# A gate of softplus and erf as two ScalarE activations instead of exp, ln and a tanh of a polynomial

## The chip, the cores and the metric

The kernel runs on one core of one Trainium2 chip. The time is the device time of one execution in microseconds (us), a median over several. The profile's span, from the first to the last instruction, is about 1.8 us shorter than the time of the same execution; against the median the difference varies, since one execution alone is profiled.

The engines in the profile's words: PE is TensorE's matmuls, PEld its weight loads, DVE is VectorE, ACT is ScalarE, POOL is GpSimd. PSUM is the memory that the kernels' matmuls write their results to. The granted clock is the share of TensorE's full clock that the profile shows as granted.

## The reference

A retention layer (a linear recurrence by head) feeds a feed-forward layer whose activation is h · erf(softplus(h)).

```python
# q, k, v: (4, 8, 768, 64)     w_in: (512, 2048)   w_out: (2048, 512), weights in float64
state = gamma * state + outer(k[t], v[t])          # for every batch and head
y[t]  = scale * q[t] @ state
x = y, as (3072, 512)
h = x @ w_in
sp = np.maximum(h, 0.0) + np.log1p(np.exp(-np.abs(h)))
g = h * erf(sp)
return (g @ w_out).astype(np.float32)
```

## The kernel before

Retention is done in 24 chunks of 128 tokens, each in four steps: transposes, scores, output, state. The feed-forward part takes 512 tokens at a time, and of them groups of FG blocks of 128 hidden features. The weights come as float64 bits and are converted on the chip. The issue order is written out by hand, so each engine works through its own instructions in program order, whatever else would be ready: in the conversion shown below VectorE idled 1.44 us for GpSimd, with the copy of a hidden block next in its queue; TensorE had ended the block at 109.26 us, and its copy began at 111.68.

```python
FG = 2  # blocks of 128 hidden features that go through the activation together
# ... [cut]
    # convert(): two shifts-and-masks, a top word, a scaled low word on VectorE, and then
    nc.scalar.activation(normal, hi.bitcast(F32), AF.Abs)
    nc.gpsimd.tensor_scalar(normal, normal, F64_LEAST, 1.0, op0=ALU.is_ge, op1=ALU.mult)
    nc.gpsimd.tensor_tensor(lowf, topf, lowf, op=ALU.add)
    nc.gpsimd.tensor_tensor(to, lowf, normal, op=ALU.mult)      # [views cut]
# ... [cut]
    # ret_out(): state and value matmuls alternate for each pair of heads
    for hp in range(HP):
        if c:
            nc.tensor.matmul(p[:, hp, :], state[:, hp, :], QD[j][:, hp, :], start=True, ...)
        for s in range(2):
            nc.tensor.matmul(p[s*D:(s+1)*D, hp, :], XT["v", j][:, 2*hp+s, :], AM[j][:, s, hp, :], ...)
    nc.scalar.copy(XC[m][:, :, i * C : (i + 1) * C], p)
# ... [cut]
def hidden(g, u):        # 4 matmuls of 512 columns into PSUM, then
    nc.scalar.copy(HS[g][:, u * TCH : (u + 1) * TCH], p)

def cap(g):              # VectorE: e = min(h, 4)
def softplus(g):         # ScalarE Exp, Ln(1 + e); GpSimd: five operations that repair the rounding
def poly(g):             # VectorE: square, first step, then
    for a in ERF_R[-2:0:-1]:
        nc.vector.scalar_tensor_tensor(z, z, a, x2, op0=ALU.add, op1=ALU.mult)
def erf_tanh(g):         # ScalarE Tanh
def gated(g):            # GpSimd: g = h * tanh
def project(g):          # 4 x FG matmuls of 512 columns into 4 PSUM banks
```

The stages of one group are spread over four rounds of the loop: cap and softplus of group g, polynomial of g−1, tanh and gating of g−2, projection of g−3.

## Time and profile before

| | before |
|---|---|
| time | 1345.3 us (1343.5 to 1346.2, four runs) |
| span of the profile | 1342.4 us |
| VectorE busy | 1204.3 us, 90% |
| GpSimd busy | 876.8 us, 65% |
| TensorE busy | 905.4 us, 67%; mean granted clock 0.819 |
| ScalarE busy | 396.7 us, 30% |

Busy time of TensorE is not its work. Overlapping records count once: the 768 of the projection last 659 ns each, 506 us in all, and count as 385.6 us. And a lower clock stretches them: at half clock (granted 0.50, from 706.2 to 709.5 us) the weight loads of the projection start 0.85 us apart, at 1.00 (from 709.6 us on) 0.43. A safer measure is the interval between starts in a stretch without gaps. The page also cuts the span into 40 slices; a digit is the busy share in tenths, and in the last line the granted TensorE clock. These are slices of the kernel before, 33.6 us each:

```profile
PE   6861537347196597939669669857966969739645
...
DVE  4668998989899899998999999999999999999995
...
PEclk9676868768597897979789779969878979859877
```

VectorE is at 8 or 9 from the fourth slice on, but for the last. TensorE swings between 1 and 9, and its clock goes largely with it: where TensorE shows 3 or less, the clock shows 5 to 7, and where it shows 9, the clock shows 8 or 9.

### The profile page before, as it was taken

What the parts mean: (1) busy time and instruction counts of PE and PEld (TensorE: products, weight loads), DVE (VectorE), ACT (ScalarE), POOL (GpSimd) and SP (SyncE); (2) the same over time, 40 slices, a digit from 0 to 9 for tenths busy, and PEclk for the clock granted to TensorE, in tenths of its full rate; (3) what the DMA queues carried; (4) which work ended last, traced back from release to release, by engine and by line L of the source; (5) the groups of instructions that cost most, each with busy time, mean ns of one, the idle gap of its engine ahead of it and who ended that gap; (6) DMA issues with size and microseconds to landing.
All of it is one profiled execution on the core that took longest, in us unless ns stands there. A gap on an engine that the chain in (4) does not pass through costs nothing.

```text
span 1342.4 us, 7959 instructions
## 1 busy us (share of the span) xinstructions
PE 905.4 (67%) x2816; PEld 449.1 (33%) x2816; DVE 1204.3 (90%) x842; ACT 396.7 (30%) x453; POOL 876.8 (65%) x410
## 2 busy tenths in 40 slices
PE   6861537347196597939669669857966969739645
PEld 4531213123043343414335334323433534314212
DVE  4668998989899899998999999999999999999995
ACT  2231122222132342423233243233323324132310
POOL 5687788887766564855756657576574666666661
PEclk9676868768597897979789779969878979859877
DMA  9531021213000210101010002000000000000000
GB/s 239 133 82 48 31 55 32 70 47 78 0 17 8 63 24 8 23 1 51 20 24 9 15 9 63 16 16 8 1 8 23 1 1 0 0 31 0 0 0 31
DMA packets 89703, 43.24 MB, mean 32 GB/s; under 512 B 76096, under 2 KB 84288, under 8 KB 89664
## 3 DMA queue, kind: packets, MB, share of 16 engines
q1 hardware_dynamic: 89664, 42.74, 12.5%
q8 instruction: 22, 0.36, 0.1%
q14 instruction: 17, 0.14, 0.0%
HBM read 36.44 MB, written 6.29 MB: 32 GB/s over the span
## 4 chain that ended last, share of the span: by engine, by line
DVE 79%; POOL 7%; PE 6%; issue 4%; ACT 2%; DMA 1%; SPq 1%; POOLq 0%; DVEq 0%
DVE xx L314 56%; DVE e L311 5%; DVE xx L312 4%; DVE e L292 4%; DVE xx L315 3%; PE r L212 3%; DVE am L220 2%; POOL low L145 2%; POOL normal L144 1%; POOL w_out_sb L147 1%; DVE qd L205 1%; ACT normal L143 1%; DMA out_dram<-osb 1%; DVE state L263 1%; PE o L331 1%
## 5 line engine op out<-in xcount | busy, mean ns | idle before, releaser
L314 DVE SCALAR_TENSOR_TENSOR xx<-xx,e 128x1024 f32<-128x1024 f32 x384 | 775.5, 2020 | 13.2
L331 PE MATMUL o<-w_out_sb,g 128*128 128x512 f32 x768 | 385.6, 659 | 75.5 <-POOL g L322 52.1
L284 PE MATMUL hp<-xT,w_in_sb 128*128 128x512 f32 x768 | 360.4, 615 | 52.1 <-ACT h L288 42.1
L322 POOL TENSOR_TENSOR g<-h,xx 128x1024 f32<-128x1024 f32 x48 | 121.2, 2525 | 295.3 <-ACT xx L318 295.3
L331 PEld LDWEIGHTS o<-w_out_sb,g 128*128 128x128 f32 x768 | 159.3, 213 | 278.8 <-issue 197.8
L212 PE MATMUL r<-qT,kT 64*128 64x128 f32 x384 | 57.3, 413 | 282.1 <-DVE qd L205 163.8
L284 PEld LDWEIGHTS hp<-xT,w_in_sb 128*128 128x128 f32 x768 | 147.6, 197 | 228.2 <-issue 172.4
L306 POOL TENSOR_TENSOR sp<-sp,xx 128x1024 f32<-128x1024 f32 x48 | 153.1, 3189 | 3.8
L305 POOL TENSOR_TENSOR xx<-xx,kept 128x1024 f32<-128x1024 f32 x48 | 152.7, 3180 | 4.0
L212 PEld LDWEIGHTS r<-qT,kT 64*128 64x128 f32 x384 | 46.7, 296 | 302.7 <-DVE qd L205 167.6
L318 ACT ACTIVATE xx<-xx 128x1024 f32<-128x1024 f32 x48 | 50.7, 1057 | 320.3 <-DVE xx L315 320.0
L302 POOL TENSOR_SCALAR xx<-e 128x1024 f32<-128x1024 f32 x48 | 78.8, 1642 | 60.2 <-ACT e L297 60.2
L288 ACT COPY h<-hp 128x512 f32<-128x512 f32 x96 | 55.6, 584 | 202.2 <-PE hp L284 191.3
L304 POOL TENSOR_SCALAR kept<-kept 128x1024 f32<-128x1024 f32 x48 | 90.0, 1876 | 4.0
L143 ACT ACTIVATE normal<-w 128x512 f32<-128x512 f32 x32 | 21.4, 667 | 237.6 <-POOL w_out_sb L147 148.6
L303 POOL TENSOR_SCALAR kept<-xx 128x1024 f32<-128x1024 f32 x48 | 86.8, 1808 | 4.0
L144 POOL TENSOR_SCALAR normal<-normal 128x512 f32<-128x512 f32 x32 | 70.2, 2194 | 23.7 <-ACT normal L143 23.7
L297 ACT ACTIVATE e<-e 128x1024 f32<-128x1024 f32 x48 | 50.5, 1053 | 100.9 <-DVE e L292 100.9
L311 DVE TENSOR_TENSOR e<-sp 128x1024 f32<-128x1024 f32 x48 | 77.8, 1621 | 0.0
L220 DVE TENSOR_TENSOR am<-r,d_in 128x512 f32<-128x512 f32 x48 | 30.9, 686 | 50.6 <-PE r L212 50.6
L145 POOL TENSOR_TENSOR low<-top,low 128x512 f32<-128x512 f32 x32 | 44.2, 1382 | 48.4 <-DVE low L142 48.4
L312 DVE TENSOR_SCALAR xx<-e 128x1024 f32<-128x1024 f32 x48 | 60.4, 1258 | 1.6
(41 smaller groups left out, 822.6 us busy)
## 6 DMA issues: line engine op xcount, KB each, us to landing
w<-in_moe_w_in_dram SPq DMA_DIRECT2D x16, 512.0 KB, 3.9
w<-in_moe_w_out_dram SPq DMA_DIRECT2D x16, 512.0 KB, 3.4
q<-in_q_dram SPq DMA_DIRECT2D x24, 256.0 KB, 3.6
k<-in_k_dram SPq DMA_DIRECT2D x24, 256.0 KB, 4.7
v<-in_v_dram SPq DMA_DIRECT2D x24, 256.0 KB, 4.3
out_dram<-osb SPq DMA_DIRECT2D x24, 256.0 KB, 2.1
d_in<-decay_in_dram SPq DMA_DIRECT2D x1, 512.0 KB, 5.0
d_q<-decay_q_dram SPq DMA_DIRECT2D x1, 256.0 KB, 5.3
```

The source lines that it names most:

```text
L144: nc.gpsimd.tensor_scalar(normal, normal, F64_LEAST, 1.0, op0=ALU.is_ge, op1=ALU.mult)
L212: nc.tensor.matmul(pp[s][:, hp, :], KT[j][s * D : (s + 1) * D, hp, :], QT[j][s * D : (s + 1) * D, hp, :], start=True, stop=True,)
L284: nc.tensor.matmul(p, w_in_sb[:, kk, ft * P : (ft + 1) * P], XC[m][:, kk, :], start=(kk == 0), stop=(kk == n_k - 1),)
L303: nc.gpsimd.tensor_scalar(kept, small, 1.0, 1.0, op0=ALU.add, op1=ALU.mult)
L304: nc.gpsimd.tensor_scalar(kept, kept, -1.0, 1.0, op0=ALU.add, op1=ALU.mult)
L305: nc.gpsimd.tensor_tensor(small, small, kept, op=ALU.subtract)
L306: nc.gpsimd.tensor_tensor(SP[g], SP[g], small, op=ALU.add)
L311: nc.vector.tensor_tensor(x2, SP[g], SP[g], op=ALU.mult)
L312: nc.vector.tensor_scalar(z, x2, ERF_R[-1], None, op0=ALU.mult)
L314: nc.vector.scalar_tensor_tensor(z, z, a, x2, op0=ALU.add, op1=ALU.mult)
L322: nc.gpsimd.tensor_tensor(G[g], HS[g], XX[g], op=ALU.mult)
L331: nc.tensor.matmul(O[m][tt], G[g][:, u * TCH + tt * P : u * TCH + (tt + 1) * P], w_out_sb[:, ft, :], start=(ft == 0), stop=(ft == n_ft - 1),)
```

## The change

The intent is to take the polynomial off VectorE and the repair off GpSimd: ScalarE has Softplus and Erf as activations, 1912 ns each for a row of 2048 elements in the profile after. Around this, six further things change: groups of four blocks instead of two, the evacuation copies from PSUM on VectorE instead of ScalarE, a shorter conversion, state matmuls before value matmuls, a pipeline one group deep, and another order of loads and conversions. With them some work changes engine: the gating product goes from GpSimd to VectorE, two small products of the retention from VectorE to GpSimd.

```diff
-FG = 2
+FG = 4
 # convert()
-        nc.scalar.activation(normal, hi.bitcast(F32), AF.Abs)
-        nc.gpsimd.tensor_scalar(normal, normal, F64_LEAST, 1.0, op0=ALU.is_ge, op1=ALU.mult)
+        nc.scalar.activation(square, hi.bitcast(F32), AF.Square)
         nc.gpsimd.tensor_tensor(lowf, topf, lowf, op=ALU.add)
-        nc.gpsimd.tensor_tensor(to, lowf, normal, op=ALU.mult)            # views cut
+        nc.vector.scalar_tensor_tensor(to, square, F64_LEAST**2, lowf,    # views cut
+                                       op0=ALU.is_ge, op1=ALU.mult)
 # retention
-            nc.scalar.copy(store[j], p)
+            nc.vector.tensor_copy(store[j], p)
-                nc.vector.tensor_tensor(QD[j], p, d_q, op=ALU.mult)
+                nc.gpsimd.tensor_tensor(QD[j], QT[j], d_q, op=ALU.mult)
-        for hp in range(HP):
-            if c: (state matmul)
-            for s in range(2): (value matmul)
-        nc.scalar.copy(XC[m][:, :, i * C : (i + 1) * C], p)
+        if c:
+            for hp in range(HP): (state matmul, start=(hp == 0))
+        for hp in range(HP):
+            for s in range(2): (value matmul, start=(not c and hp == 0))
+        nc.vector.tensor_copy(XC[m][:, :, i * C : (i + 1) * C], p)
 # feed-forward
-        nc.scalar.copy(HS[g][:, u * TCH : (u + 1) * TCH], p)
-    (cap, softplus, poly, erf_tanh)
+        nc.vector.tensor_copy(HS[g][:, u * TCH : (u + 1) * TCH], p)
+    def gate(g):
+        E[g] = act.tile([P, N], F32, name="e")
+        nc.scalar.activation(E[g], HS[g], AF.Softplus)
+        nc.scalar.activation(E[g], E[g], AF.Erf)
     def gated(g):
-        nc.gpsimd.tensor_tensor(G[g], HS[g], XX[g], op=ALU.mult)
+        for a in range(2):
+            half = slice(a * N // 2, (a + 1) * N // 2)
+            nc.vector.tensor_tensor(E[g][:, half], HS[g][:, half], E[g][:, half], op=ALU.mult)
 # loop: prologue converts 4 blocks (was 8); then, for each group
+            for u in range(FG):
+                hidden(g, u)
+                if u == 0 and g:
+                    gated(g - 1)
+                ret_step()
+                for _ in range(2):
+                    convert_piece()
+            gate(g)
+            project(g - 1)
 # [cut: order of the loads and of the pieces, w with 4 buffers, output copies all on ScalarE, the state's decay on GpSimd]
```

More of the change, by code (lines that the diff above doesn't have):

```diff
@@ L21 @@
 TCH = 512
-FG = 2
+FG = 4
 F64_LEAST = float(np.array(897 << 20, np.uint32).view(np.float32))
-H_CAP = 4.0
-ERF_R = (
-    1.128379178523394,
-    0.10277216167188301,
-    -0.00020663606065076897,
-    -0.0005953413444015755,
-    6.935073696802299e-05,
-    1.3126385158198855e-06,
-    -1.285398332234825e-06,
-    1.5565170067658438e-07,
-    -8.4325147215839e-09,
-    1.7770446978797262e-10,
-)
 @with_exitstack
@@ L88, in load @@
         b, c = divmod(j, NC)
-        for name, src in (("q", q), ("k", k), ("v", v)):
+        for name, src in (("k", k), ("q", q), ("v", v)):
             x = loads.tile([P, H, D], F32, name=name)
@@ L99 @@
     w_out_sb = const.tile([P, n_ft, d_model], F32, name="w_out_sb")
-    load(0)
-    nc.sync.dma_start(d_k, decay_k)
-    nc.sync.dma_start(d_in, decay_in)
-    nc.sync.dma_start(d_q, decay_q)
-    nc.sync.dma_start(d_s, decay_s)
     W = {}
     def load_weight(which, ft):
-        w = raw.tile([P, d_model], I64, name="w", bufs=3)
+        w = raw.tile([P, d_model], I64, name="w", bufs=4)
         if which == "in":
@@ L132, in convert @@
         low = raw.tile([P, d_model], U32, name="low")
-        normal = raw.tile([P, d_model], F32, name="normal", bufs=1)
+        square = raw.tile([P, d_model], F32, name="square")
         topf, lowf = top.bitcast(F32), low.bitcast(F32)
@@ L142, in convert @@
         nc.vector.scalar_tensor_tensor(lowf, lo, 2.0**-52, lowf, op0=ALU.mult, op1=ALU.mult)
-        nc.scalar.activation(normal, hi.bitcast(F32), AF.Abs)
-        nc.gpsimd.tensor_scalar(normal, normal, F64_LEAST, 1.0, op0=ALU.is_ge, op1=ALU.mult)
+        nc.scalar.activation(square, hi.bitcast(F32), AF.Square)
         nc.gpsimd.tensor_tensor(lowf, topf, lowf, op=ALU.add)
         g = to.shape[1]
-        nc.gpsimd.tensor_tensor(
+        nc.vector.scalar_tensor_tensor(
             to,
+            square.rearrange("p (g f) -> p g f", g=g),
+            F64_LEAST**2,
             lowf.rearrange("p (g f) -> p g f", g=g),
-            normal.rearrange("p (g f) -> p g f", g=g),
-            op=ALU.mult,
-        )
-    pieces = [("in", ft) for ft in range(n_ft // 2)]
-    for n in range(n_ft // 2):
-        pieces += [("in", n_ft // 2 + n), ("out", n)]
-    pieces += [("out", ft) for ft in range(n_ft // 2, n_ft)]
+            op0=ALU.is_ge,
+            op1=ALU.mult,
+        )
+    pieces = [("in", ft) for ft in range(FG)]
+    for n in range(n_g):
+        for u in range(FG):
+            if n + 1 < n_g:
+                pieces.append(("in", (n + 1) * FG + u))
+            pieces.append(("out", n * FG + u))
     to_load, to_convert = list(pieces), list(pieces)
@@ L167, in convert_piece @@
             load_piece()
+    load(0)
+    nc.sync.dma_start(d_k, decay_k)
+    nc.sync.dma_start(d_q, decay_q)
+    load_piece()
+    nc.sync.dma_start(d_in, decay_in)
+    nc.sync.dma_start(d_s, decay_s)
     load(1)
@@ L177 @@
     make_identity(nc, ident)
-    one = const.tile([P, 1], F32, name="one")
-    nc.vector.memset(one, 1.0)
     state = const.tile([P, HP, P], F32, name="state")
@@ L227, in ret_out @@
         p = ps_r.tile([P, HP, C], F32, name="r")
-        for hp in range(HP):
-            if c:
+        if c:
+            for hp in range(HP):
                 nc.tensor.matmul(
                     p[:, hp, :], state[:, hp, :], QD[j][:, hp, :],
-                    start=True, stop=False, skip_group_check=True,
+                    start=(hp == 0), stop=False, skip_group_check=True,
                 )
+        for hp in range(HP):
             for s in range(2):
@@ L236, in ret_out @@
                     p[s * D : (s + 1) * D, hp, :], XT["v", j][:, 2 * hp + s, :], AM[j][:, s, hp, :],
-                    start=not c, stop=True, skip_group_check=True,
+                    start=(not c and hp == 0), stop=True, skip_group_check=True,
                 )
-        nc.scalar.copy(XC[m][:, :, i * C : (i + 1) * C], p)
+        nc.vector.tensor_copy(XC[m][:, :, i * C : (i + 1) * C], p)
     def ret_state(j):
@@ L256, in ret_state @@
         if c:
-            nc.vector.tensor_tensor(
+            nc.gpsimd.tensor_tensor(
                 state, state, d_s[:, :, None].to_broadcast([P, HP, P]), op=ALU.mult
@@ L272, in ret_step @@
             f(j)
-    HS, EX, XX, SP, G, O = {}, {}, {}, {}, {}, {}
+    HS, E, O = {}, {}, {}
     def hidden(g, u):
@@ L280, in hidden @@
         if u == 0:
-            HS[g] = act.tile([P, N], F32, name="h", bufs=3)
+            HS[g] = act.tile([P, N], F32, name="h")
         p = ps_h.tile([P, TCH], F32, name="hp")
@@ L287, in hidden @@
             )
-        nc.scalar.copy(HS[g][:, u * TCH : (u + 1) * TCH], p)
-    def cap(g):
-        EX[g] = act.tile([P, N], F32, name="e")
-        nc.vector.tensor_scalar(EX[g], HS[g], H_CAP, None, op0=ALU.min)
-    def softplus(g):
-        e = EX[g]
-        nc.scalar.activation(e, e, AF.Exp)
-        SP[g] = act.tile([P, N], F32, name="sp")
-        nc.scalar.activation(SP[g], e, AF.Ln, bias=one, scale=1.0)
-        small = act.tile([P, N], F32, name="xx", bufs=3)
-        kept = act.tile([P, N], F32, name="kept", bufs=1)
-        nc.gpsimd.tensor_scalar(small, e, 1.0, 0.0, op0=ALU.min, op1=ALU.max)
-        nc.gpsimd.tensor_scalar(kept, small, 1.0, 1.0, op0=ALU.add, op1=ALU.mult)
-        nc.gpsimd.tensor_scalar(kept, kept, -1.0, 1.0, op0=ALU.add, op1=ALU.mult)
-        nc.gpsimd.tensor_tensor(small, small, kept, op=ALU.subtract)
-        nc.gpsimd.tensor_tensor(SP[g], SP[g], small, op=ALU.add)
-        XX[g] = small
-    def poly(g):
-        x2, z = EX[g], XX[g]
-        nc.vector.tensor_tensor(x2, SP[g], SP[g], op=ALU.mult)
-        nc.vector.tensor_scalar(z, x2, ERF_R[-1], None, op0=ALU.mult)
-        for a in ERF_R[-2:0:-1]:
-            nc.vector.scalar_tensor_tensor(z, z, a, x2, op0=ALU.add, op1=ALU.mult)
-        nc.vector.scalar_tensor_tensor(z, z, ERF_R[0], SP[g], op0=ALU.add, op1=ALU.mult)
-    def erf_tanh(g):
-        nc.scalar.activation(XX[g], XX[g], AF.Tanh)
+        nc.vector.tensor_copy(HS[g][:, u * TCH : (u + 1) * TCH], p)
[3 more added lines that the diff above has]
+        nc.scalar.activation(E[g], E[g], AF.Erf)
     def gated(g):
-        G[g] = act.tile([P, N], F32, name="g")
-        nc.gpsimd.tensor_tensor(G[g], HS[g], XX[g], op=ALU.mult)
+        for a in range(2):
+            half = slice(a * N // 2, (a + 1) * N // 2)
+            nc.vector.tensor_tensor(E[g][:, half], HS[g][:, half], E[g][:, half], op=ALU.mult)
     def project(g):
@@ L331, in project @@
                 nc.tensor.matmul(
-                    O[m][tt], G[g][:, u * TCH + tt * P : u * TCH + (tt + 1) * P], w_out_sb[:, ft, :],
+                    O[m][tt], E[g][:, u * TCH + tt * P : u * TCH + (tt + 1) * P], w_out_sb[:, ft, :],
                     start=(ft == 0), stop=(ft == n_ft - 1),
@@ L337, in project @@
                 o = act.tile([P, d_model], F32, name="osb")
-                if tt % 2:
-                    nc.vector.tensor_copy(o, O[m][tt])
-                else:
-                    nc.scalar.copy(o, O[m][tt])
+                nc.scalar.copy(o, O[m][tt])
                 t0 = m * TCH + tt * P
@@ L346 @@
         ret_step()
-        if i % 2:
+        if i % 4 == 1:
             convert_piece()
     NG = NM * n_g
-    for g in range(NG + 3):
-        live = g < NG
-        for u in range(FG):
-            if live:
+    for g in range(NG + 1):
+        if g < NG:
+            for u in range(FG):
                 hidden(g, u)
-            ret_step()
-        if live:
-            cap(g)
-        if 0 <= g - 2 < NG:
-            erf_tanh(g - 2)
-            gated(g - 2)
-        if live:
-            softplus(g)
-        if 0 <= g - 1 < NG:
-            poly(g - 1)
-        if 0 <= g - 3:
-            project(g - 3)
-        for _ in range(3):
-            convert_piece()
+                if u == 0 and g:
[4 more added lines that the diff above has]
+            gate(g)
+        else:
+            gated(g - 1)
+        if g:
+            project(g - 1)
 _INS = ["q", "k", "v", "moe_w_in", "moe_w_out"]
```

## The prediction

> **What bounds the kernel now.** I read the engine totals first, then the chain that ended last, then the groups that carry it, then TensorE's order of time.
>
> ```profile
> PE 905.4 (67%) x2816; PEld 449.1 (33%) x2816; DVE 1204.3 (90%) x842; ACT 396.7 (30%) x453; POOL 876.8 (65%) x410
> ...
> DVE 79%; POOL 7%; PE 6%; issue 4%; ACT 2%; DMA 1%; SPq 1%; POOLq 0%; DVEq 0%
> ...
> L314 DVE SCALAR_TENSOR_TENSOR xx<-xx,e 128x1024 f32<-128x1024 f32 x384 | 775.5, 2020 | 13.2
> ...
> L306 POOL TENSOR_TENSOR sp<-sp,xx 128x1024 f32<-128x1024 f32 x48 | 153.1, 3189 | 3.8
> ```
>
> VectorE is busy 1204 of 1342 us and is 79% of the chain; one line, the polynomial's Horner step, is 775.5 us of it, with no idle time ahead of it. So VectorE bounds the kernel. The step's mean is 2020 ns, but one line's own view gives it a minimum of 1224 and a maximum of 3273 ns for one shape: the slow ones fall beside GpSimd's two-input operations.
>
> The next question is what stands behind VectorE. TensorE's order of time shows two stretches without a gap:
>
> ```profile
> 1206.97 7.03 PE L284 MATMUL hp<-xT,w_in_sb 128*128 128x512 f32 x16
> 1213.84 7.03 PE L331 MATMUL o<-w_out_sb,g 128*128 128x512 f32 x16
> 1220.70 7.03 PE L284 MATMUL hp<-xT,w_in_sb 128*128 128x512 f32 x16
> 1227.57 7.03 PE L331 MATMUL o<-w_out_sb,g 128*128 128x512 f32 x16
> 1234.43 7.03 PE L284 MATMUL hp<-xT,w_in_sb 128*128 128x512 f32 x16
> ```
>
> ```profile
> 548.27 1.16 PE L212 MATMUL r<-qT,kT 64*128 64x128 f32 x16
> 549.36 7.13 PE L331 MATMUL o<-w_out_sb,g 128*128 128x512 f32 x16
> 556.33 3.60 PE L284 MATMUL hp<-xT,w_in_sb 128*128 128x512 f32 x8
> 559.86 1.09 PE L235 MATMUL r<-am,v 128*64 128x128 f32 x16
> 560.88 1.55 PE L284 MATMUL hp<-xT,w_in_sb 128*128 128x512 f32 x3
> ```
>
> From start to start, 64 records take 27.46 us: 0.429 us each (the 659 and 615 ns in the table overlap). Each 512-column matmul of the program is two records. Those 1536 records alone need 659 us, far above what any other engine will have left.
>
> [...]granted clock 1.00 over the 34 us from 1207, 0.52 at 707 to 709.6 us, after an idle stretch. [...]The trace has 1283 ns for each load and 1053 to 1057 ns for Exp and Tanh on 1024[...]; Softplus and Erf it does not show. [...]The trace has 1.22 us for the undisturbed 1024 steps, and 0.69 us for the two-input steps on 512.[...]
>
> **The change part by part.**
>
> *Removed.* Per 1024 elements: cap, square, ten polynomial steps (VectorE), five repair operations and the gating product (GpSimd), Exp, Ln, Tanh with their loads. On VectorE that is 51.9 + 77.8 + 60.4 + 775.5 + 58.8 = 1024 us, on GpSimd 683 us.
>
> *VectorE after.* 96 hidden copies and 72 retention copies from PSUM at 0.69 us (the row of the output copy, 688 ns): 116; 48 half products at 1.22: 59; 48 score products at 0.65: 31; 40 state updates at 0.42: 17; 32 weight conversions at 0.42 + 0.69 + 0.43 + 0.69 undisturbed, plus a new 0.69 us selection: 93. Sum 316 us, a quarter of before. GpSimd keeps about 110 us: with so little of it, the undisturbed durations are the ones to use.
>
> *ScalarE after.* Per group of 2048: two loads at 1.28 and two activations at 1.92[...], 6.4 us; 24 groups, 154 us, plus squares and output copies, about 190.
>
> *TensorE after.* Per group 32 + 32 records at 0.429 = 27.46 us, and four retention steps: transposes 0.87, scores 1.09 (548.27 to 549.36 above), output 1.03 for the values (559.86 to 560.88) plus 8 x 0.107 for the state part, state 0.89: 4.8 us. Before, state and value matmuls alternated and took 3.05 us together; separated I estimate 1.95. Sum 32.3 us. TensorE becomes the bound, by a factor of over two over VectorE.
>
> **The timeline, added up.** The order in which the changed kernel issues, with its waits, shows what a group must wait for.
>
> 1. Prologue. Four retention chunks, one conversion each. The chain is transposes, copies, scores, products, outputs, state. At the clock of 0.63 granted there now, it repeats every 14 us. I get 12.2: second transpose 1.06, copy 0.9, scores 2.8, products 1.5, output 3.8 (less 0.7 beside the products), state 2.1, update 0.9. First chunk to 17.6, hidden matmuls begin at 17.6 + 3 x 12.2 = 54 us (61.3 now), first block done at 58.
>
> 2. Groups 0 to 2 convert eight blocks each, on VectorE in program order. Here VectorE waits for GpSimd's add (1.27 us, undisturbed) in the middle of each: 2.23 + 1.3 + 0.75 + gaps = 4.45 us, eight are 35.6. Its own copies and products add 7.2, from group 1 also 2.4 of gating. So 43 + 45 + 45 = 133 us, more than TensorE's 32: VectorE still bounds here. Group 3 converts four, 36 us mostly on TensorE. First block of group 4 done at 58 + 133 + 36 = 227, begun at 224.
>
> 3. Groups 4 to 19, TensorE-bound. Gating comes after the next group's first hidden block, 17 us after softplus could start; it needs 0.2 + 5.1, so ScalarE is hidden. But VectorE does copy 0.7, gating 2.4, two transposes' copies 1.4 before scores may begin, 4.7 us, while TensorE has only 4.3 to do: a stall of 0.8 with the semaphores. 33.1 us x 16, less 4 for chunks without a state part: 525. Reaches 749.
>
> 4. Groups 20 to 23 have no retention: 4 x 27.46 = 110, to 859. Last projection 13.7, then 3.9 from the last matmul to the end as now (1338.5 to 1342.4): 877.
>
> 5. The timed median is 3 us over the span: 880. I add 10 for waits that I did not see: **890 us**.
>
> **The rivals.**
>
> *TensorE is slowed by its own density.* Now it gets 0.82 on average and is often idle; afterwards it would be dense for some 650 us. [...]I give it 4%.
>
> *The ring of waits replaces VectorE's load.* Two PSUM banks for hidden blocks and two for retention, and all evacuations now in one strict queue on VectorE, where ScalarE took most of them. If each of the four retention steps stalled by 1 us in place of only one by 0.8, groups 4 to 19 would cost 50 us more: 940. For it: the list of waits now has TensorE waiting 164 us for a VectorE product before scores. Against: those waits were behind sixteen-microsecond polynomials; afterwards the longest thing in front is 2.4 us.
>
> *ScalarE's table switching becomes the bound.* [...]6.4 us per group against 33 leaves it four fifths idle. Only if Softplus took over four times the length of Exp would it show. 2%.
>
> *The conversion stage is longer.* If contention lasts (the trace has conversion steps of 1.63 us in place of 0.69), 5.5 us in place of 4.45 for 24 conversions adds 25 us. If it is shorter because waits overlap, TensorE's 33 us bounds and up to 35 us go.
>
> **Range and chances.** Below 845 there is hardly room: 659 + 24 x 4.5 for retention is 767 us of TensorE, and the prologue's 54 and the tail's 4 have little beside them. What could fall away of the 890 is mostly stage 2's excess and my allowance: low 858. High 950 covers stalls of 1 us per step, or contention plus half of it. Faster by over 2% needs less than 1318 us: 0.99; the rest is a failure that I don't foresee.
>
> **What would show it right or wrong.** TensorE near 770 us counted by start intervals and over 95% busy from about 230 us on, clock 0.95 or more there; the chain mostly on TensorE's L273 and L297, where it was VectorE. VectorE near 320 us plus its in-order idling, product halves at 1.22 us. Softplus and Erf 1.92 us each on 2048, loads 1.28. The first hidden matmul near 54 us; group intervals near 45 us up to 190 us, then 33, then 27.5. It is wrong if the groups from 4 on repeat at more than 35 us (which wait, the list of waits says), or if the clock in them is below 0.9.

## The result, and the profile after

The changed kernel takes 873.58 us (872.8 to 874.3, four runs) against 1345.31. The ratio is 0.649 (95% interval 0.648 to 0.650). Ratios here are the mean time of one kernel's fast runs over that of the other's of the same rounds, so not quite the ratio of the medians that are quoted.

These are lines of the changed kernel's page: busy time, slices of 21.8 us, the chain that ended last, and the groups by line (busy us, mean ns of one, then idle time before them and its releaser).

```profile
PE 806.5 (93%) x2816; PEld 407.7 (47%) x2816; DVE 313.2 (36%) x465; ACT 189.3 (22%) x153; POOL 105.7 (12%) x94
...
PE   5676587878999999999999999999999999999998
...
DVE  4657767676313313313313312322322322211030
...
PEclk9798698989999999999999999999999999999999
...
PE 72%; DVE 19%; POOL 5%; issue 3%; DMA 1%; SPq 0%; ACT 0%; POOLq 0%; ACTq 0%; DVEq 0%
...
L273 PE MATMUL hp<-xT,w_in_sb 128*128 128x512 f32 x768 | 358.1, 612 | 3.7 <-DVE xT L228 3.0
L297 PE MATMUL o<-w_out_sb,e 128*128 128x512 f32 x768 | 333.4, 592 | 0.0
...
L277 DVE COPY h<-hp 128x512 f32<-128x512 f32 x96 | 66.3, 691 | 436.8 <-PE hp L273 436.4
L282 ACT ACTIVATE e<-h 128x2048 f32<-128x2048 f32 x24 | 45.9, 1912 | 462.9 <-DVE h L277 462.8
...
L288 DVE TENSOR_TENSOR e<-h,e 128x1024 f32<-128x1024 f32 x48 | 56.6, 1220 | 5.6 <-ACT e L283 5.2
...
L282 ACT ACT_TABLE_LOAD x24 | 30.8, 1283 | 0.4
```

The bound has moved from VectorE to TensorE. From the eleventh slice on TensorE is full and its clock is at its top; the busy time by stretch gives 1.00 for everything from 230 us to the end. The idle times have turned round as well: VectorE and ScalarE now wait over 400 us for TensorE, which cost nothing where it was tried (experiment 6: 5 us more of VectorE's work in a full group, 32.65 us from projection to projection in place of 32.8), and the projection (L297) has no idle time before it at all. What is left are the first ten slices, about 218 us, in which VectorE shows 4 to 7 and TensorE 5 to 8: neither is full there. Who waits for whom is for the order of time and the experiments to show.

The full part first. This is the order of time of TensorE and VectorE in one group of the changed kernel (start, duration, engine, line; in brackets the idle time before and what ended it); weight loads, ScalarE and GpSimd are left out:

```profile
418.62 3.60 PE L273 MATMUL hp<-xT,w_in_sb 128*128 128x512 f32 x8
...
422.26 0.69 DVE L277 COPY h<-hp 128x512 f32<-128x512 f32 x1 [16.24 <-PE hp L273]
...
422.93 3.60 PE L273 MATMUL hp<-xT,w_in_sb 128*128 128x512 f32 x8
422.98 2.36 DVE L288 TENSOR_TENSOR e<-h,e 128x1024 f32<-128x1024 f32 x2
...
425.25 0.69 DVE L188 COPY kT<-r 128x512 f32<-128x512 f32 x1
...
425.86 0.68 DVE L188 COPY qT<-r 128x512 f32<-128x512 f32 x1
...
426.59 1.16 PE L198 MATMUL r<-qT,kT 64*128 64x128 f32 x16
...
427.69 3.70 PE L273 MATMUL hp<-xT,w_in_sb 128*128 128x512 f32 x8
...
431.22 1.05 PE L218 MATMUL r<-qd,state 128*128 128x128 f32 x8
...
432.21 1.10 PE L224 MATMUL r<-am,v 128*64 128x128 f32 x16
...
433.23 3.70 PE L273 MATMUL hp<-xT,w_in_sb 128*128 128x512 f32 x8
```

VectorE does copy, gating, copy, copy from 422.26 to 426.54, and the scores start at 426.59. TensorE's second hidden block, started at 422.93, takes 8 x 0.429 = 3.43 us, to 426.36. So TensorE waits 0.2 us for VectorE, once in the group. ScalarE's part is seen just before, in the same view:

```profile
404.89 13.90 PE L297 MATMUL o<-w_out_sb,e 128*128 128x512 f32 x32
404.92 1.91 ACT L282 ACTIVATE e<-h 128x2048 f32<-128x2048 f32 x1 [16.82 <-DVE h L277]
...
406.85 1.28 ACT L283 ACT_TABLE_LOAD   x1
...
408.15 1.91 ACT L283 ACTIVATE e<-e 128x2048 f32<-128x2048 f32 x1
```

Softplus, one load and Erf run from 404.92 to 410.06 us, wholly beside the 13.7 us in which TensorE projects the group before. From Softplus's end to Erf's start it is 1.32 us, of which the load takes 1.28. Such a load stands before each Softplus and each Erf, 48 in the 24 groups.

The other part is the conversion stage. This is one conversion in the same view of the changed kernel:

```profile
107.30 0.42 DVE L113 TENSOR_SCALAR low<-w 128x512 uint32<-128x512 uint32 x1
...
108.94 0.69 DVE L120 SCALAR_TENSOR_TENSOR low<-w,low 128x512 f32<-128x512 uint32 x1
...
109.78 1.26 POOL L122 TENSOR_TENSOR low<-top,low 128x512 f32<-128x512 f32 x1 [3.12 <-DVE low L120]
111.08 0.69 DVE L124 SCALAR_TENSOR_TENSOR w_out_sb<-square,low 128x512 f32<-128x512 f32 x1 [1.44 <-POOL low L122]
111.68 0.68 DVE L277 COPY h<-hp 128x512 f32<-128x512 f32 x1
```

The selection (L124) stands behind GpSimd's add, and VectorE, in program order, idles 1.44 us for it; the copy of the hidden block that TensorE finished earlier comes after it. A conversion takes 111.68 − 107.30 = 4.38 us, and each of the first three groups has eight of them.

### The profile page after: what moved, and what is told of

Its sections match the earlier page's. It is cut to its first block, busy times and chain, and to the rows that moved or that the text cites. A ratio compares the mean times of both kernels' runs of the same rounds, so it can differ in the third digit from the quotient of the medians.

```text
span 871.0 us, 6926 instructions
## 1 busy us (share of the span) xinstructions
PE 806.5 (93%) x2816; PEld 407.7 (47%) x2816; DVE 313.2 (36%) x465; ACT 189.3 (22%) x153; POOL 105.7 (12%) x94
## 4 chain that ended last, share of the span: by engine, by line
PE 72%; DVE 19%; POOL 5%; issue 3%; DMA 1%; SPq 0%; ACT 0%; POOLq 0%; ACTq 0%; DVEq 0%
PE o L297 35%; PE hp L273 29%; POOL low L122 4%; DVE e L288 4%; DVE top L116 2%; PE r L224 2%; PE r L198 2%; DVE low L120 2%; DVE h L277 2%; PE r L218 2%; PE r L238 2%; DVE qT L188 1%; DVE low L119 1%; DVE w_out_sb L124 1%; DVE w_in_sb L124 1%
## 5 line engine op out<-in xcount | busy, mean ns | idle before, releaser
L297 PE MATMUL o<-w_out_sb,e 128*128 128x512 f32 x768 | 333.4, 592 | 0.0
L297 PEld LDWEIGHTS o<-w_out_sb,e 128*128 128x128 f32 x768 | 144.8, 190 | 176.5 <-issue 176.0
L277 DVE COPY h<-hp 128x512 f32<-128x512 f32 x96 | 66.3, 691 | 436.8 <-PE hp L273 436.4
L282 ACT ACTIVATE e<-h 128x2048 f32<-128x2048 f32 x24 | 45.9, 1912 | 462.9 <-DVE h L277 462.8
L191 POOL TENSOR_TENSOR qd<-qT,d_q 128x512 f32<-128x512 f32 x20 | 25.8, 1289 | 323.4 <-DVE qT L188 323.4
L288 DVE TENSOR_TENSOR e<-h,e 128x1024 f32<-128x1024 f32 x48 | 56.6, 1220 | 5.6 <-ACT e L283 5.2
L198 PE MATMUL r<-qT,kT 64*128 64x128 f32 x384 | 32.5, 316 | 20.7 <-DVE qT L188 19.9
L283 ACT ACTIVATE e<-e 128x2048 f32<-128x2048 f32 x24 | 45.9, 1912 | 0.3
L218 PE MATMUL r<-qd,state 128*128 128x128 f32 x160 | 24.1, 299 | 14.5 <-DVE am L206 14.5
L224 PE MATMUL r<-am,v 128*64 128x128 f32 x384 | 31.7, 310 | 5.2 <-DVE am L206 5.2
L224 PEld LDWEIGHTS r<-am,v 128*64 128x64 f32 x384 | 24.6, 154 | 11.2 <-DVE am L206 6.9
```

What stands on the lines that cost most here:

```text
L198: nc.tensor.matmul(pp[s][:, hp, :], KT[j][s * D : (s + 1) * D, hp, :], QT[j][s * D : (s + 1) * D, hp, :], start=True, stop=True,)
L224: nc.tensor.matmul(p[s * D : (s + 1) * D, hp, :], XT["v", j][:, 2 * hp + s, :], AM[j][:, s, hp, :], start=(not c and hp == 0), stop=True, ...
L277: nc.vector.tensor_copy(HS[g][:, u * TCH : (u + 1) * TCH], p)
L282: nc.scalar.activation(E[g], HS[g], AF.Softplus)
L283: nc.scalar.activation(E[g], E[g], AF.Erf)
L288: nc.vector.tensor_tensor(E[g][:, half], HS[g][:, half], E[g][:, half], op=ALU.mult)
```

## The experiments

The changed kernel was timed in an earlier set than the experiments, where the kernel before stood at 1345.3; in the experiments' sets it stood at 1343.8 to 1343.9, so a difference from 873.6 carries an uncertainty of about 1 us from this. Experiments 1 to 8 ran on one chip, 9 to 11 on another. "First copies" below are the starts of the first hidden block's copy of groups 0 to 4; in the changed kernel they are 54.57, 97.90, 142.43, 187.00 and 227.65 us.

Theory: the activation swap frees VectorE, and TensorE then bounds; of the remaining loss, most is the conversion stage, where VectorE's program order sets the pace. Rivals: the gain needs the rest of the change (copies, groups of four, new conversion); ScalarE's table loads or the ring of waits between VectorE and TensorE become the new bound.

### 1. The activation alone

The kernel before, with groups of two, its own copies, conversion, issue order and gating on GpSimd; only cap, repair, polynomial and tanh are replaced.

```diff
-    (cap, softplus, poly, erf_tanh)
+    def gate(g):
+        EX[g] = act.tile([P, N], F32, name="e", bufs=3)
+        nc.scalar.activation(EX[g], HS[g], AF.Softplus)
+        nc.scalar.activation(EX[g], EX[g], AF.Erf)
-        nc.gpsimd.tensor_tensor(G[g], HS[g], XX[g], op=ALU.mult)
+        nc.gpsimd.tensor_tensor(G[g], HS[g], EX[g], op=ALU.mult)
```

> The kernel before with nothing changed but the activation: Softplus and Erf on ScalarE in place of exp, ln, repair, polynomial and tanh, the one gating product still on GpSimd; groups of two blocks, copies on ScalarE, old conversion and old retention order stay. Theory (the bound moves to TensorE as soon as the polynomial is gone, and all the rest is second order): 61 us of prologue, 659 us of 512-column records, about 113 us of retention, 20 us of conversion on GpSimd, 5 us of tail and some waits: 870 us, between 845 and 900. Rival (the groups of four, or the copies on VectorE, are needed, since ScalarE then has two loads for each 1024 and all copies in one queue): over 920 us. Also expected: chain on TensorE, TensorE clock 1.00 after the first 250 us.

Measured 887.9 us (887.0 to 888.9), ratio 0.661, within the theory's range. The chain of this run, by engine:

```profile
PE 81%; POOL 10%; ACT 4%; DVE 2%; issue 1%; SPq 1%; DMA 1%; ACTq 0%; POOLq 0%
```

The swap alone gives 1343.8 − 887.9 = 456 of the 472 us. With it, and nothing else, the chain moves to TensorE.

### 2. The copies on ScalarE again

```diff
-        nc.vector.tensor_copy(HS[g][:, u * TCH : (u + 1) * TCH], p)
+        nc.scalar.copy(HS[g][:, u * TCH : (u + 1) * TCH], p)
   # and likewise for kT, qT and xT
```

> The changed kernel with the hidden, kT, qT and xT copies back on ScalarE. Theory (VectorE is the bound only in the four groups that convert weights, TensorE afterwards): each converting group loses seven copies of about 0.6 us on VectorE, some 4 us of 44; four groups make 16, and the 0.2 us wait before scores in the other groups goes: 855 us, between 850 and 864. Rival (moving the copies to VectorE was part of the gain, since on ScalarE they queue behind 6.4 us of loads and activations): slower than the 873.6 us, by 16 groups x 1 us or more, 885 to 920.

Measured 848.4 us (847.7 to 848.9): 25.2 faster, where the theory had 18; it is just below the theory's range. First copies: 45.79, 82.00, 122.62, 162.60, 204.57. At group 4 the kernel is 227.65 − 204.57 = 23.1 us ahead: 8.8 of it in the prologue, which the expectation had left out, and 14.3 in the converting groups. The direction is the theory's: ScalarE was mostly idle there (11.6 to 11.7 us busy in each of the first three groups), VectorE was not (32.6 to 34.0). "Copies on VectorE" is a part of the change that costs.

### 3. The retention matmuls alternate again

The changed kernel with the old order.

```diff
-        if c:
-            for hp in range(HP): (state matmul, start=(hp == 0))
-        for hp in range(HP):
-            for s in range(2): (value matmul)
+        for hp in range(HP):
+            if c: (state matmul, start=True)
+            for s in range(2): (value matmul)
```

> The changed kernel with the retention's state and value matmuls alternating again, as before. Theory (after the first 228 us every us on TensorE is a us of the kernel): 3.05 in place of 2.0 us in each chunk with a state part, 14 such in the groups from 4 on make 14.7, and 3 in the prologue make 3 to 6: 891 us, between 886 and 896. Rival (TensorE has slack in the retention, its waits absorb this): within 3 us of 873.6.

Measured 892.8 us (891.4 to 894.6), 19.2 more than the changed kernel and as the theory has it. TensorE's order of time in this run:

```profile
409.90 0.39 PE L218 MATMUL r<-qd,state 128*128 128x128 f32 x2
410.22 0.44 PE L223 MATMUL r<-am,v 128*64 128x128 f32 x4
...
412.58 0.44 PE L223 MATMUL r<-am,v 128*64 128x128 f32 x4
412.95 3.70 PE L272 MATMUL hp<-xT,w_in_sb 128*128 128x512 f32 x8
```

The array's shape stands before the tile's: it is 128\*128 for the state part and 128\*64 for the values, and here it changes at each of these lines. From 409.90 to the next hidden block at 412.95 it is 3.05 us; in the changed kernel, from 431.22 to 433.23, 2.01 us, for the same matmuls: 1.04 us a chunk. First copies: 58.07, 101.34, 145.87, 190.43, 234.95. The two profiled executions differ by 21.8 us: 3.5 in the prologue, nothing in groups 0 to 2, 3.9 in group 3, and 14.5 after group 4's first copy, where 14 chunks have a state part (14 x 1.04 = 14.6). So a longer TensorE costs nothing in the groups that VectorE paces, and its full length where TensorE is dense. Between the two endpoints the alternating order has six more changes of shape. If the whole difference is theirs, a change costs, as an estimate, 1.04 / 6 = 0.17 us. What TensorE does at a change no record shows.

### 4. Groups of two

```diff
-FG = 4
+FG = 2
```

> The changed kernel with groups of two feature blocks. ScalarE then has 96 loads in place of 48, 61.6 us more, and 48 more fixed costs of about 0.2 us. Theory (ScalarE is hidden: softplus and erf of a group have 10.3 us of projection and hidden block before their product is due and need 3.6): 873.6 within 6 us. Rival (the switching of tables is on the path, which is why four blocks were grouped): 930 to 945 us.

Measured 861.6 us (860.5 to 863.6): 12 faster, a miss. The rival, by which twice as many table loads cost, had 930 or more and is refuted; the theory, by which they cost nothing, had no gain. The first projection starts at 78.61 us, not at 120.31. In the first 230 us TensorE then gets 142 + 112 = 254 records of 512 columns done (hidden + projection), against 140 + 96 = 236. That is 18 x 0.429 = 7.7 us of work that does not remain for later; the two profiled executions differ by 871.0 − 861.8 = 9.2. Long groups hold back work that TensorE could do while VectorE converts; experiment 7 tests this.

### 5. The selection one conversion later

VectorE should not stand behind GpSimd's add. The selection of a conversion is kept back and issued in the middle of the next one.

```diff
+    pending = []
+    def finish():
+        if pending:
+            to, square, lowf, g = pending.pop(0)
+            nc.vector.scalar_tensor_tensor(to, square, F64_LEAST**2, lowf, ...)
     # convert(): after GpSimd's add
-        nc.vector.scalar_tensor_tensor(to, square, F64_LEAST**2, lowf, ...)
+        finish()
+        pending.append((to, square, lowf, g))
     # convert_piece(): once nothing is left to convert
+        else:
+            finish()
```

> The changed kernel with the last step of each weight conversion (the selection that waits for GpSimd's add) issued one conversion later. Theory (groups 0 to 2 are bound by VectorE's queue, of whose 4.45 us per conversion 1.4 are that wait): eight conversions save 11 us, the groups fall from 44.5 us to TensorE's 33 to 37, group 3 from 40.7 to 36: 30 us in all, 843 us, between 836 and 852. Rival (those groups are bound by something else, such as weights that arrive late or TensorE at half clock): less than 8 us gained.

Measured 850.3 us (849.9 to 851.0): 23.3 faster. First copies: 49.80, 86.06, 124.91, 163.46, 204.78. The first three groups shrink from 43.3, 44.5 and 44.6 us to 36.3, 38.9 and 38.6, and the prologue by 4.8. So VectorE's wait paced the first three. The fourth (group 3) was to fall to 36 and stays (40.65, then 41.3): TensorE still waits 2.8 us there for a copy and 2.7 us for a product of VectorE (5.2 and 4.0 in the changed kernel). Why it is not shorter all the same was not tested.

### 6. More work on VectorE

Four spare products of 1024 columns in each group, 4 x 1.22 = 4.9 us, whose results nobody uses.

```diff
+            for a in range(4):    # half: the first or the second, in turn
+                nc.vector.tensor_tensor(spare, HS[g][:, half], HS[g][:, half], op=ALU.mult)
             gate(g)
```

> The changed kernel with four more half products per group on VectorE, 4.9 us into a tile that nobody reads, after the group's last copy: 24 x 4.9 = 117 us of VectorE work. Theory (VectorE is on the path only in groups 0 to 2): 3 x 4.9 = 15 us, 888 us, between 882 and 894. Rival A (VectorE's queue is still the bound in all groups): 980 to 990. Rival B (it bounds nowhere): within 3 us of 873.6.

Measured 886.3 us (885.3 to 887.0), 12.7 more, as the theory has it. First copies: 55.45, 103.64, 153.06, 202.53, 241.63. The first three groups grow by 4.9 us each, the fourth does not, and groups from 4 on repeat as before: 32.8 us from projection to projection in the changed kernel, 32.65 here, with 5 us more on VectorE in each. It is the mirror image of the fifth experiment: after a group's last copy VectorE can take 5 us more for nothing, except in groups 0 to 2. For the groups from 4 on this refutes a ring of waits between VectorE and TensorE.

### 7. Groups of four, projection in two halves

To tell the earlier projection from the shorter group: activations on groups of four as in the changed kernel, but the first half of the projection is issued after the second hidden block.

```diff
-    def project(g):
-            for u in range(FG):
+    def project(g, part):
+            for u in range(part * FG // 2, (part + 1) * FG // 2):
 # loop
+                if u == 1 and g:
+                    project(g - 1, 0)
             gate(g)
-            project(g - 1)
+            project(g - 1, 1)
```

> The changed kernel with its groups of four, but each projection in two halves, the first issued after the next group's second hidden block. It asks why groups of two gained 12 us where none was expected. Theory (smaller portions of projection reach TensorE earlier, between conversions, where it would otherwise stand idle; by 230 us the kernel with groups of two had issued 254 records of 512 columns, the changed one 236): as groups of two, 861, between 856 and 866. Rival (it is the smaller activations, or the order of conversions, that helps): 870 to 876.

Measured 867.9 us (867.3 to 868.3): 5.7 faster, between the ranges of the theory and the rival, and in neither. The first projection starts at 104.54 us, and 144 + 101 = 245 records are done by 230 us: 9 more than in the changed kernel, half of what groups of two gave, for half the gain. The same account fits all three kernels. That the missing half is the still later start is argued from these counts, not tested by itself.

### 8. The kernel before without its repair on GpSimd

How much of the time before was VectorE's own work, and how much was GpSimd's presence? The five repair operations are deleted; the result is less exact on purpose (it still passes).

```diff
-        nc.gpsimd.tensor_scalar(small, e, 1.0, 0.0, op0=ALU.min, op1=ALU.max)
-        (two more tensor_scalar, the subtraction and the addition to SP[g])
```

> The kernel before without the five repair operations on GpSimd (so softplus is a little less exact on purpose). No VectorE instruction is removed. Theory (the Horner step's 2020 ns in place of 1224 are contention with GpSimd): its mean falls below 1350 ns, 384 x 0.7 = 270 us and some more from square and first step: 1040 us, between 990 and 1080. Rival (the steps take that long by themselves): mean over 1900 ns and a time over 1280 us.

Measured 1100.0 us (1099.3 and 1100.8), ratio 0.819. The step's mean is 1279 ns, below 1350 as expected; the time lies 20 us above the expected range and 60 above the 1040. The Horner step in the view of one line (minimum, median and maximum in ns), first in the kernel before, then without the repair:

```profile
L314 DVE SCALAR_TENSOR_TENSOR xx<-xx,e x384: 1224/1940/3273, 100.1 to 1322.7; 128x1024 f32<-128x1024 f32 x192
```

```profile
L308 DVE SCALAR_TENSOR_TENSOR xx<-xx,e x384: 1224/1226/3276, 93.8 to 1078.4; 128x1024 f32<-128x1024 f32 x192
```

No instruction of VectorE was removed, and yet the median falls from 1940 to 1226 ns, and the 384 steps from 775.5 to 491.3 us. The maximum stays at 3.28 us: GpSimd's gating product is still there. It now falls beside the square (80.0 us in all, 77.8 before; 3.38 us beside GpSimd, 1.22 undisturbed) and the first step (74.6, before 60.4): no gain there, where some was expected. That is the smaller part of the miss. VectorE's busy time fell by 288 us (1204.3 to 916.4) and the span by 245 (1342.4 to 1097.5): the other 43 us are idle time of VectorE, whose busy share fell from 90% to 83%, while TensorE's share of the chain rose from 6% to 30%. The trace of the kernel before agrees with the cause: the 126 Horner steps that overlapped no GpSimd instruction took 1.23 us on average, those mostly beside the repair's one-input operations in L303 and L304 1.94 us, and those beside its last addition 3.25 us.

### 9. Copies on ScalarE and the later selection together

Experiments 2 and 5 in one kernel: no new edit, both diffs as shown there.

> The changed kernel with both amendments that gained: copies on ScalarE and the conversion's last step issued one conversion later. Theory (each only takes VectorE's queue out of the way in the prologue and the converting groups, and TensorE is a floor under both): with copies on ScalarE the first blocks of groups 0 to 4 were copied at 45.8, 82.0, 122.6, 162.6 and 204.6 us; TensorE's own 33 to 34 us in place of 36 to 42 makes the last of them 182: 826 us, between 818 and 834. If the gains of 25 and 23 us simply added up, as a rival that sees no floor has it, it would be 825 too, so the place tells more than the sum: TensorE should stand idle or at half clock for less than 25 us after the prologue.

Measured 836.1 us (834.7 to 838.0), just outside. The gains were 25.2 and 23.3 alone and 37.5 together, so they overlap: both had shortened the prologue, by 8.8 and 4.8 us, and together they shorten it by 8.8. First copies: 45.74, 82.31, 119.63, 155.76, 192.25. The converting groups still take 36 to 37 us, more than TensorE's 32, with the granted clock at 0.81 between 45 and 100 us. From the first hidden matmul to group 4's first copy TensorE was idle or at half clock for 38.5 us, where the theory wanted under 25.

### 10. All three

Experiments 2, 4 and 5 in one kernel, with the diffs shown there.

> The same with groups of two as well. Theory (TensorE is nearly busy through the converting groups already, so an earlier first projection has little left to fill): 3 to 8 us less than with two amendments, 820 us, between 810 and 830. Rival (the gains are independent and add up): 12 us less, 813 or under. From the sums, TensorE at full clock needs about 767 us, the prologue and the tail leave it idle some 30: under 797 it can't be.

Measured 821.8 us (821.0 to 823.6), ratio 0.612 of the kernel before, and 821.8 / 873.6 = 0.941 of the changed kernel. The busy line of its page:

```profile
PE 785.9 (96%) x2816; PEld 396.1 (48%) x2816; DVE 219.4 (27%) x345; ACT 352.3 (43%) x417; POOL 114.3 (14%) x94
```

It beats both kernels. TensorE is busy 96% of the span. The time lies in the theory's range, but the step from the ninth experiment is 14 us, where I had 3 to 8: it is nearer to the rival's 12, the gain of groups of two alone. The theory that little is left to fill is not supported. Besides the earlier projection (62.24 us), the granted clock between 45 and 100 us is 0.94 instead of 0.81: work that fills a gap seems to be paid twice, once by itself and once by the clock. The two were not separated.

### 11. The activation and the order of the retention matmuls

The first experiment, with the state matmuls ahead of the value matmuls.

```diff
-        for hp in range(HP):
-            if c: (state matmul, start=True)
-            for s in range(2): (value matmul, start=not c)
+        if c:
+            for hp in range(HP): (state matmul, start=(hp == 0))
+        for hp in range(HP):
+            for s in range(2): (value matmul, start=(not c and hp == 0))
```

> The kernel before with the new activation, as in the first of these runs (887.9 us), and with the new order of the retention's state and value matmuls, nothing else. Theory (these two are the whole gain of the change; copies on VectorE, groups of four, the new conversion and prologue give and take about nothing together): 19 us less than 887.9 as the order gave there, 869, between 863 and 876. Rival (the rest of the change carries some of the gain): over 880.

Measured 864.3 us (863.9 to 866.1), ratio 0.643. These two parts alone beat the whole change by 9 us. So the rest of the change, taken together, costs 9 us instead of earning something. Experiments 2 and 4 show where: each of these two undoes one part of the rest, and gains 25 and 12 us. That is more than 9, so some other part of the rest should earn. Experiment 10 says the same: it keeps the new conversion, prologue and pipeline, and is 42.5 us faster than this kernel. The later selection gained 23.3 of this where it was tested; some 19 us (an estimate) are left for parts that no run tests alone.

## Why the prediction was right

The time, 873.6 us, lies in the range and 16.4 below the predicted 890. By its steps:

- **What is removed, and the engine sums.** Right. VectorE 313.2 us (316 predicted), ScalarE 189.3 (190), GpSimd 105.7 (110); half products 1.220 us, Softplus and Erf 1.912 us, loads 1.283, hidden copies 0.691. The 1.92 us for Softplus and Erf were an estimate, as the kernel before runs neither. On 1024 elements, in experiment 10, they take 1.057 us, so the second 1024 add 0.855; and 2 x 1.057 − 1.912 = 0.20 us is the fixed cost that the expectation of experiment 4 counts. Sums of undisturbed durations held here; experiment 8 shows how much the disturbance was. One reading was incomplete: the Horner steps were slow not only beside GpSimd's two-input operations, but also, at 1.94 us, beside its one-input ones.
- **Step 1, prologue: 4.7 us too long.** Hidden matmuls began at 49.28 us, not at 54. The term that failed is the time of a chunk: the chunks came every 10.5 to 11.5 us instead of 12.2 (the terms listed for it even add up to 12.4). The likely reason is the clock: I had taken the durations at 0.63, from the stretch 33 to 61 us of the kernel before, where the changed kernel got 0.84. No run separates this from the changed order of work.
- **Step 2, conversion.** 4.38 us each (4.45) as a rule, groups 43.3, 44.5, 44.6 (43, 45, 45). That VectorE's program order sets them, experiments 5 and 6 show from both sides. Group 3 took 40.65 us, not 36, for which the prediction gives no sum. The trace has: TensorE waits 5.2 us for VectorE's copy and 4.0 us for its product, so that the output starts 15.2 us into the group; then come the output 3.5, a hidden block 3.7, the state 0.9, the projection 13.7 and the next hidden block 3.4, which is 40.4 in all. So the step that failed here is "mostly on TensorE": the first 15 us still went at VectorE's pace. This and step 1 cancel by luck: group 4 began at 224.02 us, predicted 224.
- **Step 3, the sixteen groups bound by TensorE.** 224.02 to 743.4, 519.4 us for 525. The wait before the scores was 0.2 us, not 0.8: I had given VectorE 4.7 us ahead of the scores, where it takes 4.3, and the semaphores 0.4 as an estimate, where the scores start 0.05 us after the last copy's end. TensorE's own work was 0.3 us longer than the 32.3, so a full group repeats at 32.8, not 33.1.
- **Step 4, four groups without retention, and the tail.** 27.46 us each, 13.7 and 3.8 (3.9): as predicted.
- **Step 5, the addition of 10 us for waits that I did not see.** They came to nothing in sum. Of the 16.4 us, 10 are this allowance, 5.6 step 3, and the rest rounding and the gap of 3 us between span and time, which was 2.6 between this profile and the median.
- **The rivals.** That density would slow TensorE was a guess that no trace showed: the clock was 1.00 over the 34 us from 1207 us in the kernel before, and here it stayed at 1.00 over the 644 us from 227 us on. The ring of waits came to 0.2 us a group, and experiment 6 shows room for 5 us more. Table loads doubled in experiment 4 and the kernel got faster. (The "four times the length of Exp" has no sum: with the prediction's own 17 us of room and 5.3 of need, Softplus could have grown by 11.7 us, to some seven times its 1.9; an estimate.) Longer conversion steps came only now and then: 3 of 32 took 1.64 us in place of 0.69, and 7 of the 32 selections 1.51.

What the prediction did not ask is which parts of the change earn. It priced the change as a whole. Two parts alone give all of it and 9 us more: the activation (456 us, experiment 1) and the separated order (19 to 24 us, experiments 3 and 11). Copies on VectorE cost 25 us (experiment 2), and groups of four cost 12 (experiment 4), most of it within the first 230 us. What the conversion, the prologue and the pipeline earn or cost was not tested. The prediction had VectorE bound the converting groups, but did not ask whether the copies belonged on it there.

## What to carry to other kernels

An engine with a share of 36% over the span can still set the time in one stage: work out each stage by itself, and give movable work to the engine that is idle in that stage (the copies on ScalarE gained 25.2 us). Where an engine works in program order, put an instruction that waits for another engine later, behind work that is ready (the later selection gained 23.3 us), and let the dense engine's work start early, in small groups (groups of two gained 12 us). When a change bundles several edits, test the one that carries the idea alone: here the others together took back some of what two of them gave.
